# A gated feed-forward kernel behind attention: weight rows decoded in pairs, a start list with other durations, and the third dense chunk's steps moved forward in the second chunk

## The chip, the cores and the metric

The kernel runs on one core of one Trainium2 chip. The metric is the device time of one execution in microseconds (us). The engines are PE (TensorE: matrix products), DVE (VectorE), ACT (ScalarE), POOL (GpSimd) and SP (SyncE, which here only issues transfers). Every engine works through its own list of instructions strictly in order, and waits on semaphores for the others. "Granted clock" is the share of full speed that the chip gave PE in a stretch: 1.00 is 2.4 GHz, 0.50 is 1.2 GHz.

## The reference

Attention over batch 8, heads 8, 576 tokens, head width 64, in two parts that are added: attention between tokens averaged in fours (144 by 144, repeated four times), and a local band of seven neighbours. The result is the input x (4608 tokens by 512) of an RMS norm and a gated feed-forward layer:

```python
def _attn_ref(q, k, v):
    q_d = q.reshape(B, H, Sd, 4, D).mean(axis=3)      # k_d, v_d alike
    out_up = np.repeat(sm_attn(q_d, k_d, v_d), 4, axis=2)
    mask = np.abs(pos[:, None] - pos[None, :]) < 4
    scores = np.where(mask, scale * (q @ k.transpose(0, 1, 3, 2)), -1e9)
    ...
    return out_up + attn @ v

def _moe_ref(x, w_gate, w_val, w_out, rms_g):         # 512 -> 1536 -> 512
    xn = x / np.sqrt(np.mean(x * x, axis=-1, keepdims=True) + 1e-06) * rms_g
    g = xn @ w_gate
    return (g / (1 + np.exp(-g)) * (xn @ w_val)) @ w_out
```

The weights arrive as 64-bit floats; everything is to come out at about float32 precision.

## The kernel before, in words

**Chunks.** The tokens are worked in 18 chunks of 256. For each chunk PE runs twelve blocks f of 128 hidden columns: `first(f, 0)` and `first(f, 1)` are the gate and the value products (24 matmuls of 128x256 on L1358 in all, both into one PSUM bank of the pool `ps_h`, which has three), and `second(f)` adds the block to the output (six matmuls of 128x512 on L1394, two blocks later). Three matmuls stand for one product because each operand is split into a high part and a rest. Between `first` and `second` lie tanh (ACT, L1366), gate and product (DVE, L1369 and L1374), the high part (ACT, L1380) and the rest (DVE, L1383).

**Weights.** Each row block of weights (128x512 values, 512 KB, 36 of them) is fetched by SP (L256) and decoded once by five operations: scale (ACT, L260), last bits (ACT L268 or DVE L270), join (DVE, L277), high part (ACT L286 or DVE L288) and split (DVE, L291). Fetched and decoded forms share memory, in tiles whose sizes are listed in `SPLITS`; the same memory first holds raw inputs of the attention ("opened").

**Attention.** "Coarse" steps are the averaged attention of one batch and pair of heads (scores L551, exponentials L579 on ACT, turn L588, values L603). The local band is done in two ways: for chunks 0 to 2 on PE as a dense product (`Dense`; `early` is Dense(2), the third dense chunk, whose x is finished while chunk 1 runs), for chunks 3 to 17 on DVE, ACT and POOL (`Attention`; DVE's products and sums are L725 and L729, ACT's products L772). In a Dense chunk the softmax is L1137 (peak), L1141 (less), L1144 (powers), L1147 (total) and L1154 (shares); then come flips (L1163), values (L1186), the mix with the coarse part (L1220), squares, the norm by Newton steps (L1242 to L1257), the scaled x_t (L1263), its turn on PE (L1278), and x split into `xh` (ACT, L300) and `xl` (DVE, L304).

**What sets the order.** Chunk 0 and all that goes before and beside it are tasks of a list scheduler (`Plan`), each with an engine, a cost, a due time and its buffers; the order in which the plan starts tasks is the order of each engine's list. `HOP` is what it adds between engines. Where the plan expects PE to wait early on, filling matmuls are put (L472). From chunk 1 on, the loop at the end of the kernel emits work block by block (`todo`, `before`, `behind_second`), and `behind(x)` orders an instruction after x.

Of the kernel before, what the change touches and what calls it, by code (L numbers as in the profile page):

```python
# [40 lines left out]
W_BUFS = 4  # L41
# [10 lines left out]
HOP = {"PE": 0.25, "ACT": 0.2, "DVE": 0.15, "POOL": 0.2, "SP": 0.0}  # L52
# [129 lines left out]
def attn_moe_kernel(  # L182
# [34 lines left out]
    SPLITS = [(1, 1, 1, 1)] * 3 + [(2, 1, 1), (1, 1, 1, 1)] + [(3, 1)] * 4  # L217
# [13 lines left out]
    def opened_place(g, n):  # L231
        return home("opened", (g, n), SPLITS[g][n], [2 * WPC], FP32).rearrange("p i x -> p (i x)")

    def raw_piece(g, i):
        at, size, n = homes[g, i]
        return home("raw", at, size, [WPC, 2], U32)[:, n]

    def whole_piece(g, i):
        at, size, n = homes[g, i]
        return home("whole", at, size, [2, WPC], FP32R)[:, n]  # L240
# [10 lines left out]
    def load_weight(src, g, i):  # L251
        st = {}

        def fetch():
            raw = st["raw"] = raw_piece(g, i)
            fetched.append(nc.sync.dma_start(out=raw, in_=src.bitcast(U32).rearrange("p (n t) -> p n t", t=2)).ins)  # L256

        def scale():
            w = st["w"] = ffn.tile([P, WPC], FP32, name="o_sb", bufs=W_BUFS)
            nc.scalar.activation(  # L260
                out=w, in_=st["raw"].bitcast(FP32)[:, :, 1], func=AF.Prelu, scale=-2.0 ** -80, alpha=2.0 ** -32,
            )

        def last_bits(engine):
            raw = st["raw"]
            top = raw.bitcast(U16).rearrange("p n (t h) -> p n t h", h=2)[:, :, 0, 1]
            if engine == "act":
                nc.scalar.activation(out=raw[:, :, 0], in_=top, func=AF.Copy, scale=2.0 ** -13, bias=2.0 ** -14 - 0.5)  # L268
            else:
                nc.vector.tensor_scalar(  # L270
                    out=raw[:, :, 0], in0=raw[:, :, 0], scalar1=29, scalar2=None, op0=ALU.logical_shift_right,
                )

        def join():
            w = st["w"]
            bits = w.bitcast(U32)
            nc.vector.scalar_tensor_tensor(  # L277
                out=bits, in0=bits, scalar=3, in1=st["raw"][:, :, 0],
# [3 lines left out]
        def high(engine):  # L282
            piece = whole_piece(g, i)
            st["hi"], st["lo"] = piece[:, 0], piece[:, 1]
# [5 lines left out]
        def split():  # L290
            nc.vector.tensor_tensor(out=st["lo"], in0=st["w"], in1=st["hi"], op=ALU.subtract)  # L291
# [15 lines left out]

    def load_first(fg):
        return [
            load_weight(  # L310
                src[k * P:(k + 1) * P, fg * 4 * P:(fg + 1) * 4 * P], 3 * fg + k // 2, k % 2 * 2 + t,
            )
            for k in range(KT) for t, src in enumerate((w_gate, w_val))
        ]

    def load_second(f):
        return load_weight(w_out[f * P:(f + 1) * P], 3 * (f // 4) + 2, f % 4)
# [5 lines left out]
        "rms": 1,  # L323
# [50 lines left out]
    class OpeningSums:  # L374


        def __init__(self, b, half):
# [6 lines left out]
                task("ACT", 0.5, lambda t=t: self.spread_q(t, (0, 1)), (T0 + half if b else at), [got]) for t in range(2)  # L384
            ]
            self.late = [
                task("ACT", 0.5, lambda: [self.spread_q(t, (2,)) for t in range(2)], T0 + 2.0 + half, self.spread)
            ]
            used[self.g, 0] += self.late
            used[self.g, 1] += self.late  # L390
            last = got
            for j in range(1, FAC):
                last = task(
                    "DVE", 0.7, lambda j=j: self.add_qk(j), (T0 - 2.0 if b else 8.0) + 5.0 * half, [last],
# [21 lines left out]
        def load_qk(self):  # L416
            self.raw_qk = opened_place(self.g, 0)[:, :FAC * 4 * SD].rearrange("p (j x) -> p j x", j=FAC)
            nc.sync.dma_start(out=self.raw_qk, in_=qk_sum[self.b, :, :, self.half].rearrange("j p x -> p j x"))

        def spread_q(self, t, blocks):  # L420
            self.q = opened_place(self.g, 1)[:, :6 * P].rearrange("p (t c q) -> p t c q", t=2, c=3)
# [6 lines left out]
        def load_v(self):  # L428
            self.raw_v = opened_place(3, 0)[:HALF].rearrange("p (j x) -> p j x", j=FAC)
# [1202 lines left out]
```

## Time and profile before

| quantity | value |
| --- | --- |
| median of 3 runs | 1083.61 us (1082.1 to 1083.93) |
| profiled execution's own time | 1083.68 us |
| span of the profiled execution | 1081.9 us |
| PE busy | 1043.1 us (96%) |
| DVE, ACT, POOL busy | 883.4, 626.1, 173.3 us |
| chain that ended last | PE 83%, DVE 6%, DMA 5%, ACT 3% |

The profile is of one execution. Its own time is 1.78 us more than its span, the part that lies around the first and last instruction. Busy shares are means over very different stages: an opening without feed-forward work (until 57 us), chunk 0 beside the decoding (until about 130 us), the two chunks after it, and a long steady part.

### The profile page before, as it was taken

What the parts mean: (1) busy time and instruction counts of PE and PEld (TensorE: products, weight loads), DVE (VectorE), ACT (ScalarE), POOL (GpSimd) and SP (SyncE); (2) the same over time, 40 slices, a digit from 0 to 9 for tenths busy, and PEclk for the clock granted to TensorE, in tenths of its full rate; (3) what the DMA queues carried; (4) which work ended last, traced back from release to release, by engine and by line L of the source; (5) the groups of instructions that cost most, each with busy time, mean ns of one, the idle gap of its engine ahead of it and who ended that gap; (6) DMA issues with size and microseconds to landing.
All of it is one profiled execution on the core that took longest, in us unless ns stands there. A gap on an engine that the chain in (4) does not pass through costs nothing.

```text
span 1081.9 us, 23867 instructions
## 1 busy us (share of the span) xinstructions
PE 1043.1 (96%) x8849; PEld 963.5 (89%) x8849; DVE 883.4 (82%) x1987; ACT 626.1 (58%) x2308; POOL 173.3 (16%) x235
## 2 busy tenths in 40 slices
PE   7778999899999999999999999999999999999998
PEld 5567898789999999999999999999999999999997
DVE  6889737895978999999899898989899998986432
ACT  5878632843848394848294848384738383746221
POOL 3111300322121121212121212020202010111000
PEclk7799999899999999999999999999999999999999
DMA  8978614475352635353535353313132222210000
GB/s 268 341 232 276 132 34 122 92 160 101 91 122 64 144 91 122 88 121 86 127 75 131 77 131 79 100 41 105 44 105 68 75 88 67 84 37 21 1 20 20
DMA packets 70738, 113.14 MB, mean 105 GB/s; under 512 B 23566, under 2 KB 31518, under 8 KB 70622
## 3 DMA queue, kind: packets, MB, share of 16 engines
q1 hardware_dynamic: 43614, 89.72, 27.1%
q0 software_dynamic: 10016, 17.87, 10.3%
q10 hardware_dynamic: 16992, 4.03, 1.7%
q8 instruction: 69, 1.13, 0.4%
q14 instruction: 47, 0.39, 0.1%
HBM read 99.79 MB, written 11.80 MB: 103 GB/s over the span
## 4 chain that ended last, share of the span: by engine, by line
PE 83%; DVE 6%; DMA 5%; ACT 3%; issue 1%; SPq 0%; POOL 0%; DVEq 0%; POOLq 0%
PE ps_h L1358 52%; PE ps_o L1394 25%; PE ps_a L603 2%; DMA w<-in_w_gate_dram 2%; DMA w<-in_w_out_dram 1%; PE ps_a L551 1%; PE ps_a L875 1%; PE ps_a L588 1%; DMA vs<-in_v_sum_dram 1%; DVE prod L725 1%; DMA w<-in_v_sum_dram 1%; DVE sc L729 1%; ACT a_g L579 1%; DVE w L291 1%; DVE sil L1369 1%
## 5 line engine op out<-in xcount | busy, mean ns | idle before, releaser
L1358 PE MATMUL ps_h<-xh,w 128*128 128x256 f32 x3456 | 608.7, 278 | 0.0
L1358 PEld LDWEIGHTS ps_h<-xh,w 128*128 128x128 f32 x3456 | 529.3, 188 | 8.7 <-issue 1.0
L1358 PE MATMUL ps_h<-xl,w 128*128 128x256 f32 x1728 | 485.5, 281 | 6.3 <-DVE sil L1374 3.1
L1358 PEld LDWEIGHTS ps_h<-xl,w 128*128 128x128 f32 x1728 | 325.1, 188 | 17.2 <-DVE sil L1374 3.9
L1394 PE MATMUL ps_o<-w,hs 128*128 128x512 f32 x1296 | 331.6, 392 | 2.3 <-DVE hs L1383 2.2
L1394 PEld LDWEIGHTS ps_o<-w,hs 128*128 128x128 f32 x1296 | 230.1, 189 | 36.2 <-DVE hs L1383 2.6
L772 ACT ACTIVATE prod<-kv,sc 128x64 f32<-128x64 f32 x960 | 247.9, 426 | 13.3 <-DVE sc L763 9.7
L1366 ACT ACTIVATE sil<-ps_h 128x256 f32<-128x256 f32 x216 | 83.8, 388 | 230.1 <-PE ps_h L1358 217.2
L1380 ACT ACTIVATE hs<-sil 128x256 fp32r<-128x256 f32 x216 | 90.4, 420 | 137.1 <-DVE sil L1374 106.7
L779 POOL TENSOR_TENSOR prod<-sc,kv 128x256 f32<-128x256 f32 x120 | 92.4, 807 | 412.0 <-DVE sc L763 160.5
L1369 DVE SCALAR_TENSOR_TENSOR sil<-sil,ps_h 128x256 f32<-128x256 f32 x216 | 89.7, 415 | 76.6 <-ACT sil L1366 68.9
L798 DVE TENSOR_REDUCE x_t<-prod 128x128 f32<-128x896 f32 x120 | 127.3, 1074 | 19.2 <-PE ps_a L875 9.7
L725 DVE TENSOR_TENSOR prod<-q_t,kv 128x896 f32<-128x896 f32 x120 | 129.5, 1084 | 3.5 <-DMA kv<-in_k_pad_dram 3.3
L729 DVE TENSOR_REDUCE sc<-prod 128x14 f32<-128x896 f32 x120 | 128.3, 1076 | 0.0
L1383 DVE TENSOR_TENSOR hs<-sil,hs 128x256 fp32r<-128x256 f32 x216 | 93.5, 433 | 31.0 <-ACT hs L1380 30.7
L1374 DVE SCALAR_TENSOR_TENSOR sil<-sil,ps_h 128x256 f32<-128x256 f32 x216 | 89.4, 414 | 3.5 <-PE ps_h L1358 2.2
L372 POOL DMA_DIRECT2D qk<-in_qk_sum_dram x36 | 34.1, 946 | 227.6 <-DMA qk<-in_qk_sum_dram 214.2
L779 DVE TENSOR_TENSOR prod<-sc,kv 128x128 f32<-128x128 f32 x120 | 54.5, 475 | 0.6
L372 POOL DMA_DIRECT2D vs<-in_v_sum_dram x36 | 31.7, 882 | 85.4 <-DMA vs<-in_v_sum_dram 68.1
L579 ACT ACTIVATE a_g<-ps_a,m_g 72x144 f32<-72x144 f32 x120 | 43.7, 380 | 2.7 <-DVE m_g L574 2.5
L824 ACT ACTIVATE up_t<-x_t 128x128 f32<-128x128 f32 x120 | 38.3, 319 | 11.2 <-DVE x_t L814 10.2
L603 PEld LDWEIGHTS ps_a<-vs,a_g 72*72 72x72 f32 x480 | 36.4, 149 | 3.6 <-ACT a_g L596 2.6
(156 smaller groups left out, 798.4 us busy)
## 6 DMA issues: line engine op xcount, KB each, us to landing
kv<-in_k_pad_dram SPq DMA_DIRECT2D x60, 320.0 KB
kv<-in_v_pad_dram SPq DMA_DIRECT2D x60, 320.0 KB
qk<-in_qk_sum_dram POOLq DMA_DIRECT2D x36, 288.0 KB, 4.9
q_t<-in_q_band_dram SPq DMA_DIRECT2D x60, 128.0 KB
out_dram<-o_sb SPq DMA_DIRECT2D x30, 256.0 KB
vs<-in_v_sum_dram POOLq DMA_DIRECT2D x45, 144.0 KB, 3.4
w<-in_w_gate_dram SPq DMA_DIRECT2D x12, 512.0 KB
w<-in_w_val_dram SPq DMA_DIRECT2D x12, 512.0 KB
```

Of the source, the lines that this page charges most:

```text
L725: nc.vector.tensor_tensor(out=pr, in0=bcast(q[:, s0:s0 + 2], 2, NO), in1=window(k, s0), op=ALU.mult)
L729: nc.vector.tensor_reduce(out=self.sc[:, j, par, s0:s0 + 2], in_=self.pr[i], axis=AX.X, op=ALU.add,)
L772: nc.scalar.activation(out=self.pr[i][:, o, s], in_=self.v[j, par][:, s0 + s + o], func=AF.Copy, scale=p[:, s, o:o + 1],)
L779: (nc.vector if engine == "DVE" else nc.gpsimd).tensor_tensor(out=self.pr[i][:, a:b], in0=bcast(p[:, :, a:b].rearrange("p s o -> p o s"), ...
L798: nc.vector.tensor_reduce(out=self.x[j][:, s0:s0 + 2, par], in_=pr.rearrange("p o s d -> p s d o"), axis=AX.X, op=ALU.add,)
L1358: last = nc.tensor.matmul(out=self.p[f][:, t], lhsT=first_w(t, part, f, k), rhs=xi[:, k], start=(n == 0), stop=(n == 3 * KT - 1),).ins
L1366: nc.scalar.activation(out=self.sil[f], in_=self.p[f][:, 0], func=AF.Tanh, scale=0.5)
L1369: nc.vector.scalar_tensor_tensor(out=self.sil[f], in0=self.sil[f], scalar=1.0, in1=self.p[f][:, 0], op0=ALU.add, op1=ALU.mult,)
L1374: nc.vector.scalar_tensor_tensor(out=self.sil[f], in0=self.sil[f], scalar=0.5, in1=self.p[f][:, 1], op0=ALU.mult, op1=ALU.mult,)
L1380: nc.scalar.activation(out=self.hs[f][:, 0], in_=self.sil[f], func=AF.Copy)
L1383: (nc.gpsimd if engine == "POOL" else nc.vector).tensor_tensor(out=self.hs[f][:, 1], in0=self.sil[f], in1=self.hs[f][:, 0], op=ALU.subtract,)
L1394: last = nc.tensor.matmul(out=self.o[j], lhsT=lhs[:, cols], rhs=hopped(second_w(part, f)), start=(f == 0 and i == 0), stop=(f == NF - 1 an ...
```

## The change

Five things change together.

1. A decode step takes two rows: the gate and the value row of one k, or two rows of w_out. The five operations work on 128x1024 values, 18 times in place of 36; each step's two fetches come one behind the other in the plan and its operations wait for both. `SPLITS` becomes coarser, the buffers of the scaled value go from four of one row to two of a pair, and the first ten steps use the still free ends of tiles 5 to 8 instead (`spare`), so that what is fetched into those tiles later waits for them.
2. The plan's costs and hops are other numbers, and its tanh waits for the value product as well, since both lie in one PSUM bank.
3. The output's two halves lie in one buffer.
4. The softmax of the third dense chunk stands behind the last split of the decode, where the list of before had it inside the opening.
5. In chunk 1 the third dense chunk's flips, mix and turn go before blocks 1, 2 and 4 (before: 2, 4 and 7). The first eight band scores of chunk 3 are spread over chunk 1 and stand behind the norm of the third dense chunk; the next nine steps of that band attention are spread over chunk 2.

```diff
-W_BUFS = 4
+W_BUFS = 2
...
-HOP = {"PE": 0.25, "ACT": 0.2, "DVE": 0.15, "POOL": 0.2, "SP": 0.0}
+HOP = {"PE": 0.25, "ACT": 0.08, "DVE": 0.08, "POOL": 0.2, "SP": 0.0}
...
-    SPLITS = [(1, 1, 1, 1)] * 3 + [(2, 1, 1), (1, 1, 1, 1)] + [(3, 1)] * 4
+    SPLITS = [(2, 2)] * 5 + [(4,)] * 4
...
-        def fetch():
-            raw = st["raw"] = raw_piece(g, i)
-            fetched.append(nc.sync.dma_start(out=raw, in_=src.bitcast(U32).rearrange("p (n t) -> p n t", t=2)).ins)
+        def fetch(n):
+            if n == 0:
+                st["raw"] = raw_pieces(g, i)
+            src = sources[n].bitcast(U32).rearrange("p (n t) -> p n t", t=2)
+            fetched.append(nc.sync.dma_start(out=st["raw"][:, n], in_=src).ins)
 
         def scale():
-            w = st["w"] = ffn.tile([P, WPC], FP32, name="o_sb", bufs=W_BUFS)
+            if at:
+                st["w"] = opened_place(at)[:, 6 * WPC:].rearrange("p (i n) -> p i n", i=2)
+            else:
+                st["w"] = ffn.tile([P, 2, WPC], FP32, name="o_sb", bufs=W_BUFS)
...
         def split():
-            nc.vector.tensor_tensor(out=st["lo"], in0=st["w"], in1=st["hi"], op=ALU.subtract)
+            listed[:] = [nc.vector.tensor_tensor(out=st["lo"], in0=st["w"], in1=st["hi"], op=ALU.subtract).ins]
...
+    def spare(n):
+        return (6, 7, 8, 5, 6, 7, 8, 5, 6, 7)[n] if n < 10 else None
...
-            nc.vector.tensor_tensor(out=pr, in0=bcast(q[:, s0:s0 + 2], 2, NO), in1=window(k, s0), op=ALU.mult)
+            with behind(self.c == FIRST + 2 and early.normed):
+                nc.vector.tensor_tensor(out=pr, in0=bcast(q[:, s0:s0 + 2], 2, NO), in1=window(k, s0), op=ALU.mult)
...
                 for par in range(2):
-                    self.peak(par)
+                    with behind(listed[0]):
+                        self.peak(par)
...
-            return [(0.0, softmax), (0.1, self.load_up)], {2: flips, 4: mix, 7: turn}
+            return [(0.0, softmax), (0.1, self.load_up)], {1: flips, 2: mix, 4: turn}
...
-                tanh = task("ACT", 0.38, lambda f=f: self.tanh(f), soon, [first], allocs=[sil], uses=[hp])
                 val = task("PE", 1.375, lambda f=f: self.first(f, 1), at, [first], uses=[hp, *x])
+                tanh = task("ACT", 0.38, lambda f=f: self.tanh(f), soon, [val], allocs=[sil], uses=[hp])
...
-        got = task("SP", 0.45, fetch, 14.0 + 1.4 * n, used[place_], dma=0.45 * MB)
-        scaled = task("ACT", 0.67, scale, at, [got, *scaled_all[-1:]], allocs=[w])
+        got = [
+            task("SP", 0.45, lambda m=m: fetch(m), 14.0 + 2.8 * n + 1.4 * m, [*used[place_]], dma=0.45 * MB) for m in range(2)
+        ]
+        got[1].after.append(got[0])
+        scaled = task("ACT", 1.05, scale, at, [*got, *scaled_all[-1:]], allocs=[w])
...
-        join_ = task("DVE", 0.69, join, at, [scaled, bits], uses=[w], port=True)
+        join_ = task("DVE", 1.22, join, at, [scaled, bits], uses=[w], port=True)
...
-                todo += [(6.5 + 1.5 * at, step) for at, step in ahead.steps()[0][:8]]
+                todo += [(3.0 + 0.9 * n, step) for n, (_, step) in enumerate(ahead.steps()[0][:8])]
             elif ahead:
-                todo, ahead = todo[8:], None
+                todo, ahead = [(0.6 * n, step) for n, (_, step) in enumerate(todo[8:17])] + todo[17:], None
```

The order that the built programs have shows what the diff does not. Line numbers of the changed kernel are 5 to 14 higher than those of the kernel before for the same statement.

**SP at the start of the kernel.** In these rows `w` tiles take weight rows and `kv` tiles take raw values of the first dense chunk. The kernel before, from its first weight row on:

```order
L256 DMA w_0_130<-in_w_gate_dram 128x1024
L256 DMA w_1_168<-in_w_val_dram 128x1024
L256 DMA w_2_198<-in_w_gate_dram 128x1024
L256 DMA w_3_213<-in_w_val_dram 128x1024
L256 DMA w_0_244<-in_w_gate_dram 128x1024
L1035 DMA kv<-in_v_sum_dram 1x512
L1035 DMA kv<-in_v_sum_dram 3x512
```

The changed kernel, from its first weight row on:

```order
L261 DMA w_0_129<-in_w_gate_dram 128x1024
L261 DMA w_1_166<-in_w_gate_dram 128x1024
L261 DMA w_0_196<-in_w_gate_dram 128x1024
L1042 DMA kv<-in_v_sum_dram 1x512
L1042 DMA kv<-in_v_sum_dram 3x512
L1042 DMA kv<-in_v_sum_dram 60x1x512
L1042 DMA kv<-in_v_sum_dram 64x1x512
L261 DMA w_0_129<-in_w_val_dram 128x1024
```

Three gate rows now come first, and the value row that completes the first pair stands behind four `kv` transfers; four more `kv` transfers stand between it and the second pair's value row.

**DVE at the end of the decode, in chunk 0.** `w<-o_sb,w` is the split, `m_b`, `prod` and `z_b` belong to the softmax of the third dense chunk, `rms`, `rinv`, `newton` and `x_t` to the norm of the second dense chunk (Dense(1)). The kernel before, around its last split:

```order
L1256 TENSOR_TENSOR newton<-newton,rms 128x2
L1257 SCALAR_TENSOR_TENSOR rinv<-newton,rinv 128x2
L1374 SCALAR_TENSOR_TENSOR sil<-sil,ps_h 128x256
L291 TENSOR_TENSOR w_1_1876<-o_sb,w_1_1876 128x512
L1263 TENSOR_SCALAR x_t<-ps_a,rinv 128x256
L1383 TENSOR_TENSOR hs<-sil,hs 128x256
```

The changed kernel, from its last split on:

```order
L298 TENSOR_TENSOR w_0_1719<-o_sb,w_0_1719 128x2x512
L1145 TENSOR_REDUCE m_b<-prod 128x8 x2
L1393 TENSOR_TENSOR hs<-sil,hs 128x256
L1250 TENSOR_TENSOR rms<-ss 128x2
L1149 TENSOR_TENSOR prod<-prod,m_b 128x512 x2
L1251 TENSOR_SCALAR rms<-rms 128x2
L1252 TENSOR_SCALAR rinv<-rms 128x2
L1155 TENSOR_REDUCE z_b<-prod 128x8
L1255 TENSOR_SCALAR rinv<-rinv 128x2
```

The softmax of the third dense chunk (eight operations of 512 columns, four smaller ones) now lies between the last split and x_t, woven with the norm; x_t comes 26 rows behind the split. In PE's list the first turn of x_t (L1278) stands behind 228 matmuls of L1358 and eight output blocks in the kernel before, and its twin in the changed kernel behind 252 and nine.

**DVE in chunk 1.** `prod<-q_t,kv` and `sc<-prod` are band scores of chunk 3; `rms` to `x_t` is the norm of the third dense chunk. The kernel before, where the two meet:

```order
L1383 TENSOR_TENSOR hs<-sil,hs 128x256
L725 TENSOR_TENSOR prod<-q_t,kv 128x896 x2
L1242 TENSOR_TENSOR rms<-ss 128x2
L729 TENSOR_REDUCE sc<-prod 128x14 x2
L1243 TENSOR_SCALAR rms<-rms 128x2
L725 TENSOR_TENSOR prod<-q_t,kv 128x896 x2
L1244 TENSOR_SCALAR rinv<-rms 128x2
L729 TENSOR_REDUCE sc<-prod 128x14
L1369 SCALAR_TENSOR_TENSOR sil<-sil,ps_h 128x256
L729 TENSOR_REDUCE sc<-prod 128x14
```

The changed kernel, at the end of the same norm:

```order
L1263 SCALAR_TENSOR_TENSOR newton<-rinv 128x2
L1264 TENSOR_TENSOR newton<-newton,rms 128x2
L1265 SCALAR_TENSOR_TENSOR rinv<-newton,rinv 128x2
L1271 TENSOR_SCALAR x_t<-ps_a,rinv 128x256 x2
L733 TENSOR_TENSOR prod<-q_t,kv 128x896 x2
L737 TENSOR_REDUCE sc<-prod 128x14
L1379 SCALAR_TENSOR_TENSOR sil<-sil,ps_h 128x256
L624 TENSOR_TENSOR o_g<-ps_a,z_g 72x256
L737 TENSOR_REDUCE sc<-prod 128x14
```

The norm, which was strewn one small step at a time between wide score operations, now stands in one piece ahead of all of them. On PE its turn stood behind all 288 matmuls of L1358 of chunk 1 and now stands behind 120 of them; the values of the third dense chunk stood behind 120 and now stand behind 74.

## Rows read from the trace of the kernel before

**Rows 1.** Busy time by stage; columns: stretch, length, busy per engine, clock, DMA.

```profile
57.00:130.00 73.00, 63.00 (x895) 55.12 (x896) 63.19 (x151) 56.62 (x143) 17.66 (x21) 0.98 0.79 224
130.00:178.00 48.00, 47.92 (x512) 43.48 (x511) 21.68 (x50) 13.97 (x44) 0.00 (x0) 1.00 0.25 64
178.00:245.00 67.00, 58.63 (x447) 53.10 (x446) 59.59 (x129) 38.68 (x155) 14.89 (x19) 0.92 0.56 124
245.00:1077.00 832.00, 832.00 (x6369) 780.63 (x6369) 696.41 (x1555) 474.54 (x1849) 125.27 (x161) 1.00 0.32 81
```

**Rows 2.** Chain that ended last, first quarter; start us, us, what.

```profile
57.12 2.61 PE ps_h L1358 x12
...
120.00 4.39 PE ps_h L1358 x36
...
140.41 1.34 PE ps_o L1394 x6
```

**Rows 3.** PE's waits, 57 to 130 us: total, times, longest.

```profile
PE ps_a L588 <- ACT a_g L579: 2.2, 5, 1.3
PE ps_o L1394 <- DVE hs L1383: 2.2, 1, 2.2
PE ps_h L1358 <- DVE sil L1369: 1.3, 3, 0.5
PE ps_a L1278 <- DVE x_t L1263: 1.3, 1, 1.3
...
PE ps_h L1358 <- ACT sil L1366: 0.7, 2, 0.4
```

**Rows 4.** PE's waits, 130 to 245 us.

```profile
PE ps_a L588 <- ACT a_g L579: 2.8, 1, 2.8
PE ps_h L1358 <- DVE sil L1374: 2.6, 3, 1.1
PE ps_a L603 <- ACT a_g L596: 2.0, 1, 2.0
```

**Rows 5.** Busy time in two stretches of low clock.

```profile
198.00:204.00 6.00, 5.94 (x27) 4.91 (x29) 4.14 (x10) 4.67 (x19) 1.93 (x3) 0.50 0.48 104
228.00:232.00 4.00, 4.00 (x21) 3.46 (x19) 4.00 (x9) 0.17 (x1) 0.87 (x1) 0.57 0.79 144
```

**Rows 6.** DVE's groups by shape, 0 to 130 us: busy, mean ns, idle before.

```profile
L277 DVE SCALAR_TENSOR_TENSOR o_sb<-o_sb,w 128x512 uint32<-128x512 uint32 x36 | 24.0, 683 | 1.1 <-ACT w L268 1.0
L291 DVE TENSOR_TENSOR w<-o_sb,w 128x512 fp32r<-128x512 f32 x36 | 23.9, 680 | 0.4 <-ACT w L286 0.4
...
L270 DVE TENSOR_SCALAR w<-w 128x512 uint32<-128x512 uint32 x8 | 3.4, 421 | 0.6 <-DMA w<-in_w_val_dram 0.4 <-DMA w<-in_w_gate_dram 0.2
```

**Rows 7.** The page's costliest groups: the band's product.

```profile
L725 DVE TENSOR_TENSOR prod<-q_t,kv 128x896 f32<-128x896 f32 x120 | 129.5, 1084 | 3.5 <-DMA kv<-in_k_pad_dram 3.3
```

**Rows 8.** DVE's timeline at the last split: start, length, operation.

```profile
127.13 0.69 DVE L291 TENSOR_TENSOR w<-o_sb,w 128x512 fp32r<-128x512 f32 x1
127.73 0.48 DVE L1263 TENSOR_SCALAR x_t<-ps_a,rinv 128x256 f32<-128x256 f32 x1
```

**Rows 9.** DVE's waits, 57 to 130 us.

```profile
DVE sil L1369 <- PE ps_h L1358: 5.6, 3, 2.1
DVE sil L1369 <- ACT sil L1366: 1.5, 2, 1.1
```

**Rows 10.** ACT's groups by shape, 0 to 130 us.

```profile
L268 ACT ACTIVATE w<-w 128x512 uint32<-128x512 uint16 x28 | 18.8, 683 | 3.3 <-DMA w<-in_w_val_dram 3.3
```

**Rows 11.** DVE's timeline in chunk 1: start, length, operation, idle before.

```profile
169.54 2.10 DVE L725 TENSOR_TENSOR prod<-q_t,kv 128x896 f32<-128x896 f32 x2 [3.26 <-DMA kv<-in_k_pad_dram]
171.56 0.15 DVE L1242 TENSOR_TENSOR rms<-ss 128x2 f32<-128x2 f32 x1
...
191.64 0.78 DVE L1263 TENSOR_SCALAR x_t<-ps_a,rinv 128x256 f32<-128x256 f32 x2
```

**Rows 12.** SP's timeline in chunk 1.

```profile
165.74 2.60 SPq L631 DMA_DIRECT2D kv<-in_k_pad_dram  x4
```

More of the change, by code (lines that the diff above doesn't have):

```diff
@@ L383, in __init__ @@
             self.spread = [
-                task("ACT", 0.5, lambda t=t: self.spread_q(t, (0, 1)), (T0 + half if b else at), [got]) for t in range(2)
+                task("ACT", 0.72, lambda t=t: self.spread_q(t, (0, 1)), (T0 + half if b else at), [got]) for t in range(2)
             ]
             self.late = [
-                task("ACT", 0.5, lambda: [self.spread_q(t, (2,)) for t in range(2)], T0 + 2.0 + half, self.spread)
+                task("ACT", 0.73, lambda: [self.spread_q(t, (2,)) for t in range(2)], T0 + 2.0 + half, self.spread)
             ]
             used[self.g, 0] += self.late
-            used[self.g, 1] += self.late
             last = got
@@ L393, in __init__ @@
                 last = task(
-                    "DVE", 0.7, lambda j=j: self.add_qk(j), (T0 - 2.0 if b else 8.0) + 5.0 * half, [last],
+                    "DVE", 0.75, lambda j=j: self.add_qk(j), (T0 - 2.0 if b else 8.0) + 5.0 * half, [last],
                     allocs=[self.qk_buf] if j == 1 else [], uses=[self.qk_buf], port=True,
@@ L935, in plan @@
                 task(
-                    "PE", 0.7 if early else 0.5, lambda p=p: self.add_up(p), end - 40, [p.done, first[p.hp // 2] if early else values[-1]],
+                    "PE", 0.5 if early else 0.35, lambda p=p: self.add_up(p), end - 40, [p.done, first[p.hp // 2] if early else values[-1]],
                     uses=[p.og_buf, x_bufs[p.hp // 2]],
@@ L957, in plan @@
                 )
-                high = task("ACT", 0.95, lambda b=b: self.high(b), end - 7, [turn], uses=[tps, self.xh_buf])
-                low = task("DVE", 0.95, lambda b=b: self.low(b), end - 7, [high], uses=[tps, self.xh_buf, self.xl_buf])
+                high = task("ACT", 1.14, lambda b=b: self.high(b), end - 7, [turn], uses=[tps, self.xh_buf])
+                low = task("DVE", 1.12, lambda b=b: self.low(b), end - 7, [high], uses=[tps, self.xh_buf, self.xl_buf])
                 self.turned += [high, low]
@@ L1087, in turn @@
                 return last
-            return [(0.0, softmax), (0.1, self.load_up)], {2: flips, 4: mix, 7: turn}
+            return [(0.0, softmax), (0.1, self.load_up)], {1: flips, 2: mix, 4: turn}
         def plan_norms(self, b, xs, x_bufs, root, end):
-            first = task("DVE", 0.35, lambda: self.norm(0, b), end - 8, [root], uses=[xs, x_bufs[0]])
-            return [first, task("ACT", 0.38, lambda: self.norm(1, b), end - 8, [root], with_=[first], uses=[xs, x_bufs[1]])]
+            first = task("DVE", 0.48, lambda: self.norm(0, b), end - 8, [root], uses=[xs, x_bufs[0]])
+            return [first, task("ACT", 0.46, lambda: self.norm(1, b), end - 8, [root], with_=[first], uses=[xs, x_bufs[1]])]
         def scores(self, i, a):
@@ L1208, in load_up @@
             src = up_dram[0].rearrange("b k t (s g) d -> b s g (k t) d", g=UPP)
-            with behind(listed and listed[-1]):
+            with behind(listed[1]):
                 for i, (b, k) in enumerate(self.blocks):
@@ L1400, in copy @@
         def copy(self, j):
-            self.o_sb[j] = ffn.tile([P, DM], FP32, name="o_sb", bufs=W_BUFS)
+            if j == 0:
+                both = ffn.tile([P, 2, DM], FP32, name="o_sb", bufs=W_BUFS)
+                self.o_sb = {i: both[:, i] for i in range(2)}
             self.copied = nc.scalar.copy(
```

138 lines of the change are left out of this document (72 added, 66 removed).

## Prediction

> **What bounds the kernel now.** I read the busy time by stage first, then PE's waits in the two stages where PE is not full, then the clock there, and last the engines that PE waits for.
>
> The table of stages [rows 1] shows where time can be had at all. From 245 to 1077 us PE is busy 832.00 of 832 us at clock 1.00. The change leaves that work as it is: no feed-forward or attention matmul is added or dropped there. So these 832 us can only begin earlier or later; a faster DVE buys nothing in them. What can change lies before 245 us. There PE idles 73 - 63.00 = 10.0 us in the decode stage (57 to 130 us), 0.1 us from 130 to 178 and 67 - 58.63 = 8.4 us from 178 to 245 [rows 1].
>
> In the decode stage PE's longest waits are short and many [rows 3]: exponentials of coarse steps 2.2 us, the rest of hs 2.2, the PSUM bank held by the gate or by tanh 1.3 + 0.7, and the scaled x of the second dense chunk 1.3. DVE is busy 63.19 of the 73 us, so it is the next full engine [rows 1]; but of its 9.8 idle us, 5.6 are waits of the gate for PE and 1.5 for tanh [rows 9]. Each waits for the other in turn: the lists were interleaved so that neither is always ready.
>
> From 178 to 245 us three waits make 7.4 of the 8.4 us: exponentials 2.8, the product of blocks 2.6, coarse values 2.0 [rows 4]. The reader sees in DVE's timeline why they come there: the norm of the third dense chunk begins at 171.56 and its x_t only at 191.64, twenty us for a few small operations, because wide band scores of about a microsecond stand between its steps; the first of these scores waited 3.26 us for its keys [rows 11]. Chunk 2 cannot begin before that x_t. After two of these waits the clock is low: 0.50 from 198 to 204 us, 0.57 from 228 to 232 [rows 5].
>
> **The change part by part, against the profiled execution's own 1083.68 us** (span 1081.9 and 1.78 around it; the median of the runs, 1083.61, is practically the same).
>
> *Wider decode operations, on DVE.* The trace has no operation of 1024 columns on DVE. From 512 columns (683 ns) [rows 6] to 896 (1084 ns) [rows 7] a column costs 401/384 = 1.04 ns, so 1024 columns come to about 1.22 us. Two operations of 512 do not cost 1.37: behind the split that starts at 127.13 the next operation starts at 127.73, 0.60 later [rows 8]. With the same overlap of 0.08, one wide operation holds DVE for 1.14 us against 2 x 0.60 = 1.20: 0.06 saved, over 36 wide joins and splits 2.2 us. Against that, DVE's list now has 14 wide casts and bit operations where it had 18 narrow ones. A narrow one is 421 ns [rows 6], some 0.34 with the overlap, so 18 held 6.1 us; a wide one lies between 0.34 and 0.68, and at 0.6 (nearer to double, as with join and split) 14 hold 8.4, bounds 4.8 and 9.5. The sum on DVE is nil, between -3.5 and +1.2 us. ACT loses work, but the decode stage waits for ACT only in the 0.7 and 2.2 us above, so I credit none.
>
> The Trainium skill, "VectorE: DVE Perf Modes", section "The TRN2 errata", gives each vector operation a fixed part of some 150 cycles, and the section on the DRAIN says that the next one does not start until the pipe is empty; by that (an estimate from its formula, 691 ns at 512 and 1224 ns at 1024 columns) a pair would save 0.16 us and 36 pairs 5.7 us, not 2.2. The length at 512 agrees with the 680 to 683 ns of [rows 6], the non-overlap does not agree with [rows 8]; I take the rows, and keep the page's result as a rival.
>
> *Start of the feed-forward work.* Its first matmul stands at 57.12 [rows 2]. Up to x the same attention work has to be done. But a pair's operations wait for both its rows, and three gate rows and four transfers of the dense chunk now go out before the first value row. ACT already waits 3.3 us for a value row [rows 10]. I take +1.2 us, a third of that; bounds 0 (attention work covers it) and +3.3 (the whole wait again).
>
> *Decode stage.* DVE's work ahead of the second dense chunk's x_t is about equal: the softmax of the third dense chunk, eight operations of 512 columns at 0.60 = 4.8 us [rows 8] and some small ones, moves from ahead of the last split to behind it, but still stands before x_t, in all some 8 us between split and x_t where there was none. In PE's list, however, 24 matmuls and one output block more stand ahead of the turn: 24 x 4.39/36 + 1.34 = 4.3 us of work [rows 2] that covers most of those 8. So the 1.3 us wait for x_t goes if DVE comes to it about as late as before. What should shrink is the mutual waiting. With measured durations in the list, and tanh planned behind the value product where the bank forces it anyway, I expect DVE's 7.1 us of waits at the gate [rows 9] to fall to some 2, and PE's 10.0 to about 4: -6.0 us. Bounds: -9 (PE nearly full) and -1 (only the x_t wait is covered). What is late next if I am wrong is x_t itself, behind the softmax: every us by which it outlasts PE's cover is idle PE.
>
> *Chunks 1 and 2.* In the changed list the norm stands in one piece ahead of the scores, and its turn behind 120 of chunk 1's 288 matmuls instead of behind all. The 168 matmuls that now stand behind the turn are 168 x 0.122 = 20 us of cover for xh and xl [rows 2]. So chunk 2 has its x in time, and the pile-up of 178 to 235 us dissolves: scores spread over chunk 1, where DVE was busy only 21.68 of 48 us [rows 1], coarse steps apart from ACT's band products. Of the 8.4 us idle I let 1.9 stand: -6.5 us, bounds -8.4 and -2. With the waits the low clock goes. At 0.50, 5.94 busy us lose 2.97; at 0.57, 4.00 lose 1.72 [rows 5]: 4.7 at most, since small matmuls need not be bound by the clock; I take -3.5, bounds -4.7 and 0.
>
> New here: the moved scores wait for keys. In before those transfers are issued at 165.74 [rows 12], when the third dense chunk's values free the buffers, and the first score starts at 169.54 after 3.26 us of waiting [rows 11]. The values now stand 46 matmuls earlier, 5.6 us with [rows 2], and the scores come with the turn, another 46 behind the values. So the wait can return, with gate and product of a block queued behind it on DVE. Three PSUM banks hold PE over a block or so, 4.3 us; a wait of 3.26 is just covered. I cost it at nothing, bound 3.3.
>
> *Costed at nothing.* The joint output buffer: it still holds two chunks' output, and chunks are some 55 us apart (832 us [rows 1] for about fifteen), which hides the store; without that cover PE would wait for the copy at each chunk's end. The fewer filling matmuls: they run while PE waits for x anyway; the first twelve matmuls took 2.61 us where 36 later ones took 4.39 [rows 2], so the start is at low clock already and can't lose more than it does. The fetches into tiles 6 and 7, which now wait for splits 8 and 9, the last of the gate and value weights for blocks 4 to 7: four blocks of 4.3 us on PE, and the splits queued on DVE, hide them; a fetch later than that leaves DVE idle, and x_t comes later one to one.
>
> Sum: +1.2 - 6.0 - 6.5 - 3.5 = -14.8, so 1083.68 - 14.8 = 1068.9 us; I say 1069.
>
> **Rivals.**
>
> *Only chunks 1 and 2 gain* (chance 0.20). The softmax ahead of x_t, 8 us against 4.3 of cover, and the later start eat what the better interleaving gives, and the decode stage ends where it did: 1083.7 - 10.0 = 1074 us. For it speaks that DVE's total there is the same; against it, that DVE idles 9.8 us now.
>
> *Only the opening gains* (0.08). The scores in chunk 1 wait for keys or delay gates, and as much idle time arises there as goes after 178 us: 1083.7 - 4.8 = 1079 us. Against it stands DVE's half empty stretch from 130 to 178 us.
>
> *Slower* (0.07): the start. If the first pairs are held by their value rows and everything in order behind them on ACT and DVE is held too, each us passes on one to one. With the other terms at -16.0 it decides at a start of 57.1 + 16 = 73 us; at 76 the time would be 1087. For it: ACT's 3.3 us wait for one such row, now possible in each of the first three steps; 16 us would take five such waits, none covered.
>
> *No change in effect* (0.06): the list's numbers shift the order, but PE finds the same waits in other places; 1083 us. Against it, the norm's order in chunk 1 certainly differs.
>
> *Wide operations save their whole fixed part* (0.04): DVE ends its decode 3.5 us earlier than I reckon and x_t with it: 1068.9 - 3.5 = 1065 us. The 0.60 spacing [rows 8] speaks against it. The Trainium skill's page "VectorE: DVE Perf Modes" would have it so.
>
> **How the numbers follow.** The forecast has 0.55, the rivals 0.20, 0.08, 0.07, 0.06 and 0.04. The range 1061 to 1080 us takes in both half gains and the dearer ends of the start and the keys; its low end is the sum with the favourable bounds of the two stages half taken (-1.5 in the first, -2 in the second, -1.2 for the start, and the wide operations' 3.5). Outside stay the slower case, no change and a small tail, under 2 in 10. A measurement of this kernel tells about 0.2%, 2.2 us, from no change. Faster by more than that: 0.55 + 0.20 + 0.08 + 0.04 = 0.87; within it 0.06; slower 0.07.
>
> **What would show it.** First matmul of the feed-forward at 57 to 60 us. PE's idle time in the decode stage about 4 us, with waits for gate and tanh nearly gone; last split near 118 us (127.1 - 4.8 of softmax - 5.1 of gate waits + 1.2) and x_t some 8 us behind. In chunk 1 the norm takes about 3 us, not twenty, and the turn comes mid-chunk. PE at clock 1.00 from chunk 1 on, with under 2 us idle up to chunk 3, and the steady part as long as before. I am wrong if the start is over 62 us, if PE waits long for x_t at the end of the decode, or if the scores' wait for keys shows as PE's wait for product or hs in chunk 1.

## The result, and the profile after

The changed kernel took 1067.16 us in the median of 4 runs (1065.19 to 1068.43), the kernel before 1083.44; the ratio is 0.985 with a 95% interval of 0.9833 to 0.9867. 1069 us had been forecast, between 1061 and 1080. A second set of five runs gave 1067.19 us and 0.9857 (0.9834 to 0.9879). The profiled execution is the fastest of its set: 1065.19 us with a span of 1063.4, so its times lie 18.5 us below the profiled execution of before, where the medians lie 16.3 apart.

The stages of the changed kernel; columns as in [rows 1]:

```profile
57.00:130.00 73.00, 66.37 (x959) 59.24 (x960) 65.44 (x135) 51.61 (x112) 18.64 (x22) 0.98 0.78 210
130.00:178.00 48.00, 48.00 (x522) 43.61 (x521) 31.77 (x77) 17.31 (x56) 0.26 (x1) 1.00 0.32 85
178.00:245.00 67.00, 66.33 (x546) 60.96 (x546) 57.45 (x123) 43.81 (x177) 18.93 (x25) 1.00 0.63 134
```

PE is full from 130 us on but for 0.7 us, and at full clock; in the decode stage 6.6 us of idle time are left where there were 10.0. From 130 to 178 us DVE now works 31.77 us in place of 21.68: the scores went there.

Both kernels happen to issue the second dense chunk's turn at 128.36 us. So the two executions can be cut there. First the kernel before, from its first gate matmul to the turn, and from the turn to 245 us; then the changed kernel, whose first gate matmul is at 59.05, with its steady part to 1058.60 us (the last matmul ends at 1059.07):

```profile
57.12:128.36 71.24, 61.35 (x880) 53.45 (x881) 62.49 (x150) 55.21 (x139) 17.66 (x21) 0.98 0.78 225
128.36:245.00 116.64, 108.20 (x970) 98.22 (x971) 81.86 (x180) 53.94 (x204) 14.89 (x19) 0.96 0.44 100
```

```profile
59.05:128.36 69.31, 63.86 (x910) 57.14 (x911) 62.39 (x125) 48.14 (x103) 18.64 (x22) 0.98 0.79 214
128.36:240.00 111.64, 110.97 (x1043) 101.73 (x1044) 88.50 (x200) 58.38 (x221) 17.59 (x22) 1.00 0.49 112
240.00:1058.60 818.60, 818.60 (x6267) 768.19 (x6266) 689.45 (x1534) 469.77 (x1833) 122.08 (x158) 1.00 0.32 81
```

Ahead of the cut the changed kernel starts 1.9 us later but has 24 gate and value matmuls and one output block more behind it: 4.3 us of work, as worked out in the prediction. Its parts: idle time falls from 71.24 - 61.35 = 9.89 us to 69.31 - 63.86 = 5.45, that is by 4.4; the start takes 1.9 of it back; the other 1.8 are the same matmuls taking less time. Behind the cut, idle time falls from 116.64 - 108.20 = 8.44 us to 0.67. The whole difference is 18.5 us; 4.3 + 7.8 leave 6.4 us for the same matmuls running faster. The half clock of [rows 5] is at most 4.7 of these; for the other 1.7, as for the 1.8 ahead of the cut, no row was found that accounts for them. The steady part is full in both.

PE's waits of the changed kernel from 57 to 135 us, the longest:

```profile
PE ps_a L1288 <- DVE x_t L1271: 2.5, 1, 2.5
PE ps_h L1109 <- DVE xl L311: 1.5, 1, 1.5
PE ps_a L595 <- ACT a_g L586: 1.4, 2, 1.1
PE ps_h L1368 <- ACT xl L1136: 1.1, 1, 1.1
PE ps_o L1404 <- DVE hs L1393: 0.5, 1, 0.5
```

Against [rows 3]: the waits for a PSUM bank that the gate or tanh still holds, 1.3 + 0.7 us, are gone (in their place stand 1.1 us for a bank that the third dense chunk's scores hold until ACT has copied them, L1136), that for hs fell from 2.2 to 0.5, and that for x_t grew from 1.3 to 2.5. The reason for the last stands in DVE's timeline, the last split, the first softmax row behind it, and x_t:

```profile
119.18 1.22 DVE L298 TENSOR_TENSOR w<-o_sb,w 128x1024 fp32r<-128x1024 f32 x1
120.31 1.27 DVE L1145 TENSOR_REDUCE m_b<-prod 128x8 f32<-128x512 f32 x2
...
127.74 0.48 DVE L1271 TENSOR_SCALAR x_t<-ps_a,rinv 128x256 f32<-128x256 f32 x1
```

The split is 7.95 us earlier than in [rows 8], and x_t starts at the same time as there, to a hundredth of a microsecond. Of DVE's own waits from 57 to 130 us, the gate's wait for PE (5.6 us in [rows 9]) no longer appears, while that for tanh grew from 1.5 to 2.3 us; the two largest now are:

```profile
DVE sil L1379 <- ACT sil L1376: 2.3, 3, 1.5
DVE w L278 <- DMA w<-in_w_out_dram: 1.3, 1, 1.3
```

In chunk 1 the norm stands in one piece; DVE's timeline, its first operation, its x_t and the first band score:

```profile
155.14 0.16 DVE L1250 TENSOR_TENSOR rms<-ss 128x2 f32<-128x2 f32 x1 [2.74 <-ACT x_t L1241]
...
157.78 0.88 DVE L1271 TENSOR_SCALAR x_t<-ps_a,rinv 128x256 f32<-128x256 f32 x2
158.57 2.08 DVE L733 TENSOR_TENSOR prod<-q_t,kv 128x896 f32<-128x896 f32 x2
```

2.6 us from first to last, where [rows 11] show twenty; and the score behind it no longer waits for its keys.

### The profile page after: what moved, and what is told of

Same layout as the page of the kernel before. It is cut to its first block, busy times and chain, and to the rows that moved or that the text cites. A ratio compares the mean times of both kernels' runs of the same rounds, so it can differ in the third digit from the quotient of the medians.

```text
span 1063.4 us, 23847 instructions
## 1 busy us (share of the span) xinstructions
PE 1035.8 (97%) x8879; PEld 959.5 (90%) x8879; DVE 883.1 (83%) x1947; ACT 617.3 (58%) x2258; POOL 173.6 (16%) x235
## 3 DMA queue, kind: packets, MB, share of 16 engines
q0 software_dynamic: 10016, 17.87, 10.6%
q8 instruction: 69, 1.13, 0.4%
## 4 chain that ended last, share of the span: by engine, by line
PE 86%; DMA 8%; DVE 3%; ACT 1%; issue 1%; SPq 1%; POOL 0%; ACTq 0%; DVEq 0%; POOLq 0%
PE ps_h L1368 53%; PE ps_o L1404 26%; DMA w<-in_w_gate_dram 3%; PE ps_a L610 2%; DMA w<-in_w_val_dram 2%; PE ps_a L558 1%; PE ps_a L883 1%; DMA qk<-in_qk_sum_dram 1%; PE ps_a L595 1%; DMA w<-in_w_out_dram 1%; DMA min_sb<-in_band_min_dram 1%; DVE prod L733 1%; DMA q_t<-in_q_band_dram 0%; DVE w L298 0%; DVE sc L737 0%
## 5 line engine op out<-in xcount | busy, mean ns | idle before, releaser
L311 DVE SCALAR_TENSOR_TENSOR xl<-ps_a,g_sb,xh 128x128 fp32r<-128x128 f32 x136 | 37.7, 338 | 1.2 <-ACT xh L307 1.2
```

## The experiments

The theory was that two gains are independent: the opening's, from the list's other numbers, and the larger one of chunks 1 and 2, from the norm standing ahead of the scores. The rivals were that the wide decode steps bring the opening's gain, and that either gain depends on the other. All times are medians of 4 to 10 runs against the kernel before in the same session. "First gate matmul" and "253rd" are read from the profiled execution: when the first and the 253rd matmul of that line start, the latter as a measure of how far chunk 0 has come.

| kernel | us | ratio to before, 95% | first gate matmul | 253rd |
| --- | --- | --- | --- | --- |
| before | 1083.4 | | 57.1 | 135.1 |
| changed | 1067.16 | 0.985 (0.9833 to 0.9867) | 59.0 | 128.7 |
| changed, again | 1067.19 | 0.9857 (0.9834 to 0.9879) | 60.2 | 129.2 |
| moved steps only | 1070.61 | 0.9874 (0.9848 to 0.9900) | 56.8 | 136.5 |
| opening only | 1080.42 | 0.9966 (0.9947 to 0.9986) | 61.2 | 130.5 |
| list's numbers only | 1076.53 | 0.9931 (0.9909 to 0.9953) | 57.0 | 127.8 |
| narrow decode, all else | 1064.78 | 0.9824 (0.9796 to 0.9852) | 57.4 | 126.0 |
| softmax early | 1068.83 | 0.9860 (0.9832 to 0.9889) | 60.5 | 128.6 |
| softmax behind x_t | 1065.96 | 0.9841 (0.9807 to 0.9874) | 60.7 | 126.6 |
| fetches in pairs | 1068.16 | 0.9857 (0.9827 to 0.9887) | 59.7 | 129.9 |
| narrow, softmax behind x_t | 1068.09 | 0.9856 (0.9825 to 0.9887) | 59.1 | 123.4 |
| dense steps only | 1083.95 | 1.0002 (0.9988 to 1.0017) | 56.6 | 136.6 |
| numbers and moved steps | 1065.11 | 0.9833 (0.9813 to 0.9853) | 58.5 | 126.1 |
| output weights behind x | 1076.30 | 0.9927 (0.9913 to 0.9941) | 61.1 | 139.0 |

**Moved steps only.** The kernel before with the loop's part of the diff. With it go two small moves that the list of changes ahead of the prediction does not name: the third dense chunk's up-load waits for an earlier instruction, and the first coarse swap of chunk 1 comes earlier.

```diff
-            return [(0.0, softmax), (0.1, self.load_up)], {2: flips, 4: mix, 7: turn}
+            return [(0.0, softmax), (0.1, self.load_up)], {1: flips, 2: mix, 4: turn}
...
+            with behind(self.c == FIRST + 2 and early.normed):
...
-                todo += [(6.5 + 1.5 * at, step) for at, step in ahead.steps()[0][:8]]
+                todo += [(3.0 + 0.9 * n, step) for n, (_, step) in enumerate(ahead.steps()[0][:8])]
```

> The kernel before with only the moved steps of chunks 1 and 2 (third dense chunk's flips, mix and turn before blocks 1, 2 and 4, the band scores of chunk 3 spread over chunk 1 behind the norm, the first coarse swap earlier); decode, list and softmax stay as they were. Theory: the two gains are independent, and this one is the larger. PE's 8.4 us of idle time and the low clock between 178 and 245 us go, the decode stage stays with its 10 us idle; 1083.4 - 12 to 14 = 1069 to 1072 us. Rival (the moved steps only fit because the opening was re-ordered too): new waits in chunk 1, 1078 us or more.

1070.61 us, 13 below before. Its stages:

```profile
57.00:130.00 73.00, 62.65 (x883) 55.23 (x883) 62.73 (x151) 55.36 (x138) 17.64 (x21) 0.95 0.76 219
130.00:178.00 48.00, 47.93 (x521) 43.48 (x519) 27.72 (x71) 17.52 (x57) 0.00 (x0) 1.00 0.30 75
178.00:245.00 67.00, 67.00 (x557) 62.11 (x557) 61.56 (x131) 40.52 (x164) 16.80 (x22) 1.00 0.63 137
```

From 178 to 245 us PE is full at full clock, with the decode stage as it was in [rows 1]. The norm takes 2.6 us here too, and the turn stands behind 120 matmuls of chunk 1. The larger gain needs nothing of the opening.

**Opening only.** The changed kernel with those lines and moves taken back.

> The changed kernel with the steps of chunks 1 and 2 put back where they were. Theory: only the opening's gain is left, the 24 matmuls and one output block more that PE has done at the turn of the second dense chunk; 1083.4 - 4.2 = 1079 us, and PE's waits of 2.8, 2.6 and 2.0 us in chunk 1 and 2 with the half clock behind them are back. Rival (what the opening gains is given back in chunk 1 where chunk 2's x is late anyway): 1083 us.

1080.42 us, 0.34% below before. The ratios of the two halves multiply to 0.9874 x 0.9966 = 0.984, inside the changed kernel's interval: within the intervals the gains add. PE's waits from 135 to 250 us are back, and in the decode stage the 2.6 us for x_t stands as in the changed kernel:

```profile
PE ps_h L1367 <- DVE sil L1383: 4.0, 4, 2.2
PE ps_a L595 <- ACT a_g L586: 2.2, 1, 2.2
PE ps_a L610 <- ACT a_g L603: 1.1, 1, 1.1
```

**Narrow decode, all else as changed.** Decode code, tiles and buffers of before (one row a step, 36 steps).

```diff
-    SPLITS = [(2, 2)] * 5 + [(4,)] * 4
+    SPLITS = [(1, 1, 1, 1)] * 3 + [(2, 1, 1), (1, 1, 1, 1)] + [(3, 1)] * 4
...
-        scaled = task("ACT", 1.05, scale, at, [*got, *scaled_all[-1:]], allocs=[w])
+        scaled = task("ACT", 0.67, scale, at, [got, *scaled_all[-1:]], allocs=[w])
```

> The changed kernel with decode steps of one row again (36 narrow steps, tiles and buffers of before); list numbers, softmax behind the last split and moved steps as in the changed kernel. Theory: the wide operations gain nothing by themselves, since DVE's time in the decode is equal; 1066 to 1069 us, as the changed kernel, and with the start at 57 rather than 59 us perhaps 1 to 2 us better. Rival (the wide operations are what frees DVE in the opening): 1071 us.

1064.78 us. The wide steps bring no gain; the ratio's interval overlaps that of the changed kernel, so that they cost something is likely but not shown by the time alone.

**The list's numbers only.** Of the diff, the plan's costs and hops, and tanh behind the value product.

```diff
-HOP = {"PE": 0.25, "ACT": 0.2, "DVE": 0.15, "POOL": 0.2, "SP": 0.0}
+HOP = {"PE": 0.25, "ACT": 0.08, "DVE": 0.08, "POOL": 0.2, "SP": 0.0}
...
-                tanh = task("ACT", 0.38, lambda f=f: self.tanh(f), soon, [first], allocs=[sil], uses=[hp])
+                tanh = task("ACT", 0.38, lambda f=f: self.tanh(f), soon, [val], allocs=[sil], uses=[hp])
```

> The kernel before with only the list's other costs and hops, and tanh planned behind the value product. Theory: these numbers are what ends the mutual waiting of PE and DVE in the decode stage; 1083.4 - 4 = 1079 us, PE idle under 7 us from 57 to 130. Rival (the gain of the opening needs the wide steps): 1083 us with 10 us idle.

1076.53 us, 7 below before: more than the whole opening of the changed kernel gains. PE's stage row, its waits in the stage, and DVE's largest wait there (the profiled execution is the slowest of the six, 1078.87 us):

```profile
57.00:130.00 73.00, 69.68 (x937) 62.78 (x938) 65.24 (x160) 57.37 (x146) 18.61 (x22) 0.93 0.78 214
```

```profile
PE ps_a L588 <- ACT a_g L579: 2.0, 3, 1.4
PE ps_h L1358 <- DVE sil L1374: 1.1, 1, 1.1
PE ps_h L1358 <- DVE xl L304: 0.3, 1, 0.3
```

```profile
DVE sil L1369 <- ACT sil L1366: 3.2, 4, 1.4
```

3.3 us of idle time instead of 10.0, and PE does not wait for x_t: the softmax stands where it stood before. So these edits are enough to end the mutual waiting, without wide steps; which of the three does it (costs, hops or tanh's place) was not parted. The opening as a whole gains some 4 us less (0.9966 against 0.9931, with intervals that just overlap); what it has besides are the wide steps with their tiles, the joint output buffer and the softmax's place.

**Where the softmax stands.** Three kernels: the changed one without the hold behind the last split, the changed one with the hold behind the second dense chunk's x_t, and the latter with narrow decode.

```diff
-                    with behind(listed[0]):
-                        self.peak(par)
+                    self.peak(par)
```

> The changed kernel with the third dense chunk's softmax not held behind the last split, so that it stands some sixty rows earlier in DVE's list, among the decode steps. Theory: its 5 to 6 us of DVE time then delay the last splits and x_t by as much as they did behind them, since DVE's total ahead of x_t is the same; PE's 2.5 us wait for x_t becomes waits for weights, and the time stays at 1066 to 1069 us. Rival (the place behind the split is what costs the 2.5 us): 1064 us.

```diff
-                    with behind(listed[0]):
+                    with behind(atts[FIRST].normed):
```

> The changed kernel with that softmax behind the second dense chunk's x_t in place of behind the last split. Theory: x_t no longer waits for 8 us of other work, PE's 2.5 us wait goes, and chunk 1 has room for the softmax on DVE; 1067.2 - 2.5 = 1064 to 1065 us, with no new wait for the flips. Rival (the flips, which stand 48 matmuls into chunk 1, then wait for the softmax): 1067 us or more.

The same line on the kernel with narrow decode:

> Decode steps of one row, the changed kernel's list numbers and moved steps, and the softmax behind the second dense chunk's x_t. Theory: the gains add, 3.2 us of wait for x_t go from the kernel with narrow steps (1064.8 us); 1061 to 1063 us. Rival (DVE is the bound in the opening, and what x_t gains the gates of chunk 0 lose): 1065 us.

Early: 1068.83 us, no gain, as expected; the wait for x_t goes, and PE waits 1.4 us for hs (0.5 in the changed kernel), not for weights as had been expected, with a start 1.4 us later in this execution. Behind x_t, with wide steps: 1065.96 us. PE's turn stands at 126.25 without a wait although this execution began 1.6 us later than the changed kernel's, and the 253rd matmul comes 2.1 us earlier; the intervals of the two times overlap, so the gain is read from the trace and not from the times. Narrow and behind x_t: the opening is the best of all, the 253rd matmul at 123.4, and yet the time is 1068.09. The rival named for it was wrong, too: the gates of chunk 0 lost nothing. What was gained was given back in chunk 2. PE's only wait from 135 to 245 us, and the stretches around it:

```profile
PE ps_a L588 <- ACT a_g L579: 4.1, 1, 4.1
```

```profile
215.00:220.00 5.00, 1.00 (x9) 1.00 (x9) 5.00 (x9) 2.36 (x12) 0.13 (x1) 0.81 0.74 188
220.00:225.00 5.00, 5.00 (x20) 4.42 (x19) 5.00 (x12) 0.99 (x3) 0.84 (x1) 0.50 0.52 124
```

A coarse step's peaks stood on DVE behind band operations that had waited 5.35 us for a product of POOL; PE idled 4.1 us and then ran at half clock from 220 to 225 us. So in this execution the better opening was not passed on. That the loop's order in chunk 2 suits the instants at which the other kernels come to it is a reading of these rows; no run tests it.

**Dense steps only.** The kernel before with flips, mix and turn moved, but the scores of chunk 3 neither held behind the norm nor spread anew.

> The kernel before with only the third dense chunk's flips, mix and turn moved to blocks 1, 2 and 4 (with its up-load and the first coarse swap); the band scores of chunk 3 stay where they were in the loop, not held behind the norm. Theory: what matters is that the norm is over before chunk 2; its turn now stands behind 234 of 288 matmuls, so chunk 2's x is in time and most of the gain of the moved steps (13 us) is there: 1071 to 1074 us. Rival (the scores' place ahead of the norm is the cause, the steps alone leave the norm strewn between scores): 1077 us or more, with PE's waits of the stretch after 178 us still there.

1083.95 us, no change; the theory's version for this run fell and the rival held. Its DVE timeline, the norm's first and last operation:

```profile
165.44 0.15 DVE L1242 TENSOR_TENSOR rms<-ss 128x2 f32<-128x2 f32 x1
...
184.88 0.81 DVE L1263 TENSOR_SCALAR x_t<-ps_a,rinv 128x256 f32<-128x256 f32 x2
```

The norm starts 6 us earlier than in [rows 11] and still takes 19 us, since the scores stand ahead of it and between its steps as before; from 135 to 245 us PE waits 6.0 us for products and 2.2 for exponentials. By themselves the moved lines bring the turn only from behind 288 matmuls to behind 234, which is 54 x 0.122 = 6.6 us, and that gains nothing; behind 120 it stands only in the kernels that also hold and spread the scores. Those two edits together are what is needed beside the moved steps. Which of them does it, the hold behind the norm or the new spread, was not tried, nor was the turn behind 120 matmuls without them.

**Numbers and moved steps.** Both of the parts that gained, with decode and softmax as before.

> The kernel before with the list's other numbers and the moved steps; decode steps of one row and the softmax where they were. Theory: the two gains add, 0.9931 x 0.9874 = 0.981, 1062 to 1064 us, below the changed kernel, with no wait of PE for x_t at the end of the decode and the start near 57 us. Rival (the softmax inside the opening costs as much there as behind the last split): 1065 us, as with narrow steps and the softmax behind the split.

1065.11 us, beside 1067.19 of the changed kernel in the same session, with overlapping intervals. The gains add but for some 3 us (0.9806 is the product, 0.9833 came), which the intervals of the two factors cover: this execution's first gate matmul stood at 58.5, and 1.6 us of waits for coarse exponentials appear in chunk 2. The time equals that of the narrow kernel with the softmax behind the split, from which it differs by that place and by the up-load of the third dense chunk, which starts at 138.3 us here and at 133.6 there; so the rival's number came true.

**The late start.** Two kernels that try to take away why the first gate matmul comes at 59.0 to 61.2 us in the seven executions with wide steps and at 56.6 to 59.1 in the seven with narrow ones. Fetches in pairs:

```diff
-        got[1].after.append(got[0])
```

> The changed kernel with each pair's second fetch directly behind its first in SP's list (the plan's second fetch no longer waits for the first). Theory: the start at 59 us in place of 57 comes from rows that arrive late and hold ACT and DVE in order ahead of x; with the fetches in pairs the first gate matmul comes at 57 to 58 us and the time falls by 1 to 2 us to 1065 to 1066. Rival (the start is late because each wide operation stands twice as long in front of the attention's): start at 59 us, 1067 us.

1068.16 us, start at 59.7, as the rival had it. But the edit does less than it was meant to: SP issues the value rows of the first two pairs at 7.1 and 10.6 us in place of 15.1 and 20.3, that of the third only at 24.0, behind eight `kv` transfers, and up to 60 us ACT waits 7.4 us for value rows, where it waits 2.0 and 6.0 in the two profiles of the changed kernel. The late rows are not taken away, so this run does not tell its theory from its rival. First output weights behind x:

```diff
+        x_first = atts[0].turns if n == KT else []
-        scaled = task("ACT", 1.05, scale, at, [*got, *scaled_all[-1:]], allocs=[w])
+        scaled = task("ACT", 1.05, scale, at, [*got, *scaled_all[-1:], *x_first], allocs=[w])
```

> The changed kernel with the scale and last bits of the first pair of output weights planned behind the turn of the first x. Theory: the late start comes from ACT standing in order at a pair whose second row has not landed, ahead of x; without that wait (3.3 us in the changed kernel) the first gate matmul comes at 57 to 58 us; the time falls by 1 to 2 us unless the later decode gives it back. Rival (the start is late because earlier wide steps already delay the squares): start at 59 us or later.

1076.30 us, start at 61.1. ACT's wait for that row is gone (the second profile of the changed kernel, with its start at 60.2, does not have it either) and the start is not earlier, while decode work that had fitted ahead of x now comes behind it (x_t of the second dense chunk 7 us later, with 4.2 us of waiting for it). The rows that remain: ACT's squares of the first x start at 45.34 in the kernel before and at 47.92 in the changed one, 2.6 us later, and from there to the first gate matmul both take about the same, 11.8 and 11.1 us. The delay lies ahead of the squares. In the first 45 us DVE is busy 31.69 us in the kernel before and 30.44 in the changed one (27.75 in its second profile), and waits 3.1 and 5.1 us for rows of weights where it waited 0.6. That pairs wait for their second row then, is what these rows suggest. It is not shown: with fetches in pairs DVE waits 1.7 us for such rows in that time and the start is still at 59.7, the rival that a wide operation stands twice as long in front of the attention's is not ruled out, and of the narrow kernels the four with the list's new numbers start at 57.0 to 59.1 us, the three with the old ones at 56.6 to 57.1. A kernel that decodes only the first pairs narrowly was not run.

**The changed kernel again**, beside the three kernels of the last session.

> The changed kernel itself, beside the others on the same chip. Theory: 1066 to 1068 us, its first gate matmul between 59 and 61 us, and so 3 to 4 us slower than the list's numbers with the moved steps and narrow decode.

1067.19 us, as before, its start at 60.2; 2 us above the numbers with the moved steps, not 3 to 4.

## Why the prediction was right

The time was right to 2 us by the medians. Between the two profiled executions, to which the sum belongs, the change is -18.5 us against -14.8, so the terms are off by more than the time, and the misses go both ways: the start and the decode stage's idle time came out 0.7 and 1.6 us worse, the idle time behind it and the time of the same matmuls 1.3 and 4.7 us better. That the medians agree so well is partly luck. The two larger terms have the sign and, in the main, the reasons given; one small term fell.

- *Where time can be had.* Right: the steady part is full in both, and the lead reached by the third chunk stays to the end.
- *Wide operations.* Right on DVE: 1.216 us each (1.22 reckoned) with the next operation 1.13 behind the split at 119.18 (1.14), and no gain by themselves, as the narrow kernel shows. The rival that let them save their whole fixed part is out: the Trainium skill, "VectorE: DVE Perf Modes", section "The TRN2 errata", has the length right (1224 ns, an estimate by its formula). But operations overlap here by 0.09 us at 1024 columns as at 512. The Trainium skill's section "The DRAIN you can't avoid" on that page, from which the prediction took this rival, itself adds that a next operation that is not held starts earlier, which the prediction left out; the 0.09 us agree with that.

```profile
L298 DVE TENSOR_TENSOR w<-w,w 128x1024 fp32r<-128x1024 f32 x10 | 12.2, 1216 | 1.1 <-ACT w L293 1.0
```

- *Start.* +1.2 taken, +1.9 in the profile, up to +4 in others. The sign was right and the size near. Its reason, that pairs wait for their value rows, fits DVE's waits in the first 45 us (0.6 to 3.1 and 5.1) but is not shown; the cause of the later start stays open.
- *Decode stage.* -6.0 with the start's +1.2 makes -4.8; measured is 4.3 us of work ahead at the same instant. The two are near only because 1.8 us that no term had make up for idle time that fell by 4.4 instead of 6.0. The gate's waits on DVE fell from 7.1 to 2.3 us (2 reckoned), and the list's numbers with tanh's place alone bring them to 3.2: the reason held. What failed is "the 1.3 us wait for x_t goes": it grew to 2.5. The eight microseconds between split and x_t came as reckoned (119.18 to 127.74), and DVE came to x_t as late as before, which was the condition; but PE, with fewer waits ahead of it, came to the turn at 125.9 us, 1.2 earlier than before in spite of its 4.3 us of added work, so this cover was too short. The prediction had named this as what would be late next and as a sign of being wrong.
- *Chunks 1 and 2.* -6.5 of idle time, measured -7.8; -3.5 for the low clock, 4.7 at most, where the same matmuls took 6.4 us less, so that at least 1.7 of this is something that the sum did not have. The norm in one piece and the pile-up gone are as forecast. Two steps of the reasoning are weaker than they read. "Chunk 2 cannot begin before that x_t" was hardly what held PE: of the 8.4 idle us before, only the wait in the row below, at the start of chunk 2, was for that chunk's x; the others were for products and coarse steps. And the prediction did not part the moved steps from the hold and the spread of the scores: without these two the steps leave the turn behind 234 matmuls and gain nothing.

```profile
PE ps_h L1358 <- DVE xl L304: 0.9, 1, 0.9
```

- *Keys.* Costed at nothing; the first score stands at 158.57 directly behind x_t, with no wait.
- *Fills.* The prediction had fewer filling matmuls; the trace counts 93 where there were 63. They end before the first gate matmul either way (at 53.9 and 55.3 us), and no row shows an effect.

The rivals "only chunks 1 and 2" and "only the opening" are the two half kernels, 1070.61 and 1080.42 us: each gain is real, the first larger than the -10.0 and the second smaller than the -4.8 of the sum.

## What to carry to other kernels

Look for a chain of tiny dependent operations (here a norm by Newton steps) that shares an in-order engine with wide ones: strewn between them, 2.6 us of work took twenty. Moving the steps around the chain earlier in the program gained nothing by itself; with the wide operations held behind the chain and spread anew it gained 13 us, and which of these two edits did it is open. In a list scheduler, other costs and hops, and a task planned behind all that it shares a bank with, were worth 7 us without any change of the work; fewer, wider operations were worth nothing where the narrow ones already overlapped; and after a better opening it pays to look again at the chunks behind it, since a stall can come back there.

## What the runs showed of the hardware that had not been expected

The same program's first gate matmul moves by about a microsecond between executions: 59.0 and 60.2 us in two profiles of the changed kernel, whose runs lie between 1065.2 and 1073.0 us. Differences of 2 us between two such kernels are hard to tell by a few runs. In the narrow kernel with the softmax behind x_t, a stall of 4.1 us on PE was followed by five microseconds at clock 0.50 in which PE was busy all the time, so it can have cost up to 2.5 us more than its own length.
